# Float64 weights on a float32 chip: the sign set by a parametric ReLU instead of a masked OR

## The chip, the cores and the metric

The kernel runs on one core of a Trainium2 chip. The metric is device time of one execution in microseconds (us), the median over runs; before the change it is 1353.39 us over three runs (1353.15 to 1353.93). TensorE (PE in the rows) multiplies, VectorE (DVE) and ScalarE (ACT) do the elementwise work, SyncE (SP) issues the DMAs, GpSimd (POOL) does next to nothing. Each engine runs its own instructions strictly in order and waits on semaphores for the others.

## The reference

Two-way attention between a sequence and a small state, then two feed-forward layers. B = H = 8, S = 512, 32 state rows, head size 64; the layers see 4352 rows (512 + 32 rows for each of 8 batches), d_model 512, d_ff 2048.

```python
scores = scale * x @ state^T            # softmax over the state  -> xread = a @ state
scores2 = scale * state @ x^T           # softmax over the sequence -> sread = a2 @ x
x = concat(xread, sread) per head, laid out as rows of 512
h = x @ w_in;  x = (max(h, 0)**2) @ w_out              # first layer
h = x @ w_in2; x = elu(h) @ w_out2                     # second layer
```

The four weight matrices arrive as float64 (a float32 draw times a float64 factor). The chip's engines work on float32, so the kernel reads each float64 as two 32-bit words and builds a float32 from them.

## The kernel before, in words

**Stages.** The first layer runs batch by batch for six batches (`block`, 27.7 to about 505 us; it is written with plain products in three float32 pieces: a value is split into a high and a low part, and each product takes three matmuls, lines 158 to 160). Batches 6 and 7 are done as a pair with a seven-product scheme (`pair`, from about 505 us), then come the state rows and, from about 690 us, the whole second layer. Inside `block`, step i makes one tile h of 128 hidden rows (6 matmuls `h`), squares its ReLU (`relu2`, lines 469 to 474) and, two steps later, adds it into four accumulators (12 matmuls `acc`). `emit_m` folds the state into the first weight (`mp` matmuls of line 331, eight to a call) four times a batch.

**Conversion.** 64 pieces of 128 x 512 float64 (16 each of w1, v1, w2, v2) are converted beside this work. `load64` (line 195) loads a piece into one of four `raw` buffers. `convert` then runs: ACT scales the high word, read as a float32 of every second word, by 2^-112 (line 210); ACT scales the low word as an unsigned integer by 2^-29 (line 212); DVE clamps (line 214), shifts the bits left by three (line 215), which moves the float64 exponent's low bits and the mantissa into place and pushes the sign out; DVE adds the low word (line 217); and DVE ORs the sign bit of the high word back in with one scalar_tensor_tensor (line 219), which is the last reader of the `raw` buffer and the last writer of the converted piece. The pieces of w1 and v1 are all needed within batch 0; those of w2 and v2 are converted in batches 1 to 5 (`conv_pair`), where also sums of blocks (`sums`, lines 247 to 251) and splits (`put_split`, lines 260 and 261) are made and written to HBM.

**What sets the order.** `convert` and its callers are generators; each call of `next_conv` advances every conversion under way by one `yield`, starts one more, and when a conversion ends, issues the next load. In batch 0 there are two such calls a step. The layer that records the kernel then lists each engine's instructions in an order of its own, by dependencies and estimated costs; so taking one instruction out can reorder others far from it, on all engines, in both directions. Loads and stores all sit in the one queue of SP, in that recorded order.

**Start.** Until the first h matmul, PE runs the scores of batch 0, idle products that only keep it active (line 517), and the first `emit_m`, whose weight pieces come out of `convert`.

Of the kernel before, what the change touches and what calls it, by code (L numbers as in the profile page):

```python
# [9 lines left out]
F32 = mybir.dt.float32  # L10
# [3 lines left out]
AF = mybir.ActivationFunctionType  # L14
ALU = mybir.AluOpType
# [15 lines left out]
HF = FC // 2  # L31

CLAMP = 2.0 ** -96 * (2.0 - 2.0 ** -3 - 2.0 ** -22)
SIGN = -(1 << 31)
HI, LO = 0, 1
SINGLE = 6

# [67 lines left out]
def attn_mlp_kernel(ctx: ExitStack, tc: tile.TileContext, xt, xn, st, w1, v1, w2, v2, outx, outs):  # L105
# [13 lines left out]
    nc = tc.nc  # L119
# [49 lines left out]
    if True:  # L169
# [30 lines left out]
        def convert(name, i, out):  # L200

            t = raw.pop((name, i))
            low, high = t[:, :, 0], t[:, :, 1]
            bits = out.bitcast(I32)
            after = pace if name in ("w2", "v2") else gate
            with tc.issue_after(after[0].ins) if after else nullcontext():
                nc.scalar.activation(out=out, in_=high.bitcast(F32), func=AF.Copy, scale=2.0 ** -112)  # L210
            with tc.issue_after(gate[0].ins) if gate else nullcontext():
                nc.scalar.activation(out=low, in_=low.bitcast(U32), func=AF.Copy, scale=2.0 ** -29)
            yield
            nc.vector.tensor_scalar(out=out, in0=out, scalar1=CLAMP, scalar2=-CLAMP, op0=ALU.min, op1=ALU.max)
            nc.vector.tensor_single_scalar(out=bits, in_=bits, scalar=3, op=ALU.logical_shift_left)
            yield
            nc.vector.tensor_tensor(out=bits, in0=bits, in1=low, op=ALU.add)
            yield
            nc.vector.scalar_tensor_tensor(out=bits, in0=high, scalar=SIGN, in1=bits, op0=ALU.bitwise_and, op1=ALU.bitwise_or)

        def conv_w1(i):
            g, k = divmod(i, KC)
            if k % 2 == 0:
                half[g, k // 2] = wi_p.tile([P, 2, 512], F32, name=f"w1_{g}{k // 2}", tag="wi")
            t = half[g, k // 2]
            yield from convert("w1", i, t[:, k % 2])
            if k % 2:
                w1_t[g, k // 2] = t

        def conv_v1(f):  # L230
            v = conv_p["cv"].tile([P, 512], F32, name="cv", tag="cv")
            yield from convert("v1", f, v)
            d = wd["v1", f] = dram.tile([P, 512], F32, name=f"d_v1{f}", tag=f"d_v1{f}")
            nc.sync.dma_start(out=d, in_=v)
            t = wo_p.tile([P, 2, DM], F32R, name=f"v1_{f}", tag="wo")
            nc.scalar.activation(out=t[:, HI], in_=v, func=AF.Copy)
            yield
            nc.vector.tensor_tensor(out=t[:, LO], in0=v, in1=t[:, HI].bitcast(F32), op=ALU.subtract)
            wo_t["v1", f] = t
# [25 lines left out]
        def conv_pair(name, j):  # L265


            v = [conv_p["cv"].tile([P, 512], F32, name="cv", tag="cv") for _ in range(2)]
            for _ in zip_longest(convert(name, j, v[0]), convert(name, j + HF, v[1])):
                yield  # L270
            d = wd[name, j] = dram.tile([P, 2, 512], F32, name=f"d_{name}{j}", tag=f"d_{name}{j}")
            for r in range(2):
                nc.sync.dma_start(out=d[:, r], in_=v[r])
            for t in sums(v):
                yield
            w = wf[name, j] = dram.tile([P, NF, 2, 256], F32, name=f"f_{name}{j}", tag=f"f_{name}{j}")
            yield from put_split(w, ((1, v[0][:, :256].unsqueeze(1)), (2, v[1].rearrange("p (q f) -> p q f", q=2)),
                                     (2, t[:, :2]), (2, t[:, 2:])))
# [712 lines left out]
```

## Time and profile before

| what | value |
|---|---|
| median of 3 runs | 1353.39 us |
| span of the profiled execution, first to last instruction | 1350.5 us |
| mean granted TensorE clock | 0.997 |
| PE busy | 1327.5 us, 98% |
| DVE busy | 951.0 us, 70% |
| ACT busy | 839.5 us, 62% |
| DMA, mean over the span | 215 GB/s, 290.72 MB |

The page gives no time around the span of the profiled execution; the median of the runs is 2.9 us above the span. Busy shares are averages over stages that differ: DVE is at 70% over the whole, but busy 84.2 of 92.1 us in batch 0. PE at 98% leaves 23 us of the span in which it does nothing, and the question of any change off PE is how much of those 23 us it touches. The chain of work that ended last is 89% PE, 5% DMA, 3% DVE, 3% ACT.

### The profile page before, as it was taken

To read this page: it belongs to the slowest core of one execution; us is meant where nothing else is said; L and a number is where in the kernel's file an instruction comes from. 1 tells how busy PE (TensorE), PEld (TensorE's weight loads), DVE (VectorE), ACT (ScalarE), POOL (GpSimd) and SP (SyncE) were. 2 spreads that over 40 slices of the span, in tenths; PEclk is the share of its full clock that TensorE was granted. 3 is DMA by queue.
4 is the path that set the end of the run, shared out by engine and by line. 5 is a ranking of instruction groups with operands and counts; after the bars stand their busy time and mean duration, and the time that the engine had idled before them with its cause. 6 is when DMAs were issued, how large, how long until landed. Compare 5 with 4: busy or idle time off the path is not lost.

```text
span 1350.5 us, 19746 instructions
## 1 busy us (share of the span) xinstructions
PE 1327.5 (98%) x7064; PEld 1057.1 (78%) x7064; DVE 951.0 (70%) x1437; ACT 839.5 (62%) x1417; POOL 0.7 (0%) x6
## 2 busy tenths in 40 slices
PE   8989999999999999999999999999999999999998
PEld 6656777777777776778988888888888888888898
DVE  6997868686878865775576884579636884568644
ACT  5887758676777657644467843676446743666444
POOL 0000000000000000000000000000000000000000
PEclk9999999999999999999999999999999999999999
DMA  6988856575857424279077777767776777778732
GB/s 240 318 300 310 305 178 230 201 267 190 279 197 266 151 82 153 97 255 349 25 252 208 224 240 224 208 194 247 229 225 194 206 210 223 209 204 284 226 110 100
DMA packets 127729, 290.72 MB, mean 215 GB/s; under 512 B 13840, under 2 KB 22032, under 8 KB 124560
## 3 DMA queue, kind: packets, MB, share of 16 engines
q1 hardware_dynamic: 127632, 289.46, 66.3%
q8 instruction: 56, 0.92, 0.3%
q14 instruction: 41, 0.34, 0.1%
HBM read 212.86 MB, written 76.55 MB: 214 GB/s over the span
## 4 chain that ended last, share of the span: by engine, by line
PE 89%; DMA 5%; DVE 3%; ACT 3%; issue 1%; SPq 0%; ACTq 0%; DVEq 0%
PE x L43 16%; PE X L43 13%; PE z L43 8%; PE Z L43 6%; PE acc L158 6%; PE acc L159 6%; PE acc L160 6%; PE h L158 5%; PE h L159 4%; PE h L160 4%; PE y L43 4%; PE Y L43 3%; DMA raw_v<-in_v_dram 2%; PE mp L331 2%; PE hs L43 2%; PE as L43 2%
## 5 line engine op out<-in xcount | busy, mean ns | idle before, releaser
L163 ACT ACTIVATE gp<-g 128x1024 fp32r<-128x1024 f32 (+1 forms) x168 | 154.0, 917 | 146.0 <-PE x L43 69.5
L164 DVE TENSOR_TENSOR gp<-g,gp 128x1024 fp32r<-128x1024 f32 (+1 forms) x168 | 174.9, 1045 | 95.4 <-ACT gp L163 94.4
L43 PE MATMUL x<-gp,wr 128*128 128x512 f32 x960 | 223.5, 390 | 0.0
L43 PEld LDWEIGHTS x<-gp,wr 128*128 128x128 f32 x960 | 179.7, 188 | 39.4 <-ACT eu L71 1.9
L43 PE MATMUL X<-xf,wr 128*128 128x512 f32 x768 | 186.7, 390 | 0.0
L43 PEld LDWEIGHTS X<-xf,wr 128*128 128x128 f32 x768 | 143.4, 188 | 31.7 <-ACT u L748 1.3
L158 PE MATMUL acc<-gs,v 128*128 128x512 f32 x384 | 154.4, 402 | 3.8 <-DVE gs L474 1.9
L159 PE MATMUL acc<-gs,v 128*128 128x512 f32 x384 | 150.4, 392 | 0.0
L160 PE MATMUL acc<-gs,v 128*128 128x512 f32 x384 | 150.2, 392 | 0.0
L43 PE MATMUL z<-gp,wr 128*128 128x512 f32 x480 | 110.4, 389 | 0.0
L744 DVE SCALAR_TENSOR_TENSOR g<-r,g 128x512 f32<-128x512 f32 x96 | 63.9, 689 | 65.8 <-ACT r L743 65.8
L43 PEld LDWEIGHTS z<-gp,wr 128*128 128x128 f32 x480 | 90.1, 188 | 18.7
L158 PE MATMUL h<-at,m 128*128 128x512 f32 x256 | 103.0, 403 | 1.7 <-ACT r L469 1.7
L158 PEld LDWEIGHTS acc<-gs,v 128*128 128x128 f32 x384 | 72.0, 188 | 38.1 <-issue 15.9
L160 PE MATMUL h<-at,m 128*128 128x512 f32 x256 | 100.7, 395 | 0.5 <-ACT m L346 0.5
L159 PE MATMUL h<-at,m 128*128 128x512 f32 x256 | 101.0, 395 | 0.0
L43 PE MATMUL Z<-xf,wr 128*128 128x512 f32 x384 | 97.4, 389 | 0.0
L469 ACT ACTIVATE r<-h 128x512 f32<-128x512 f32 x96 | 57.1, 595 | 64.4 <-PE h L160 64.1
L742 ACT ACTIVATE r<-g 128x512 f32<-128x512 f32 x96 | 57.5, 625 | 57.5 <-DVE g L821 40.4
L160 PEld LDWEIGHTS acc<-gs,v 128*128 128x128 f32 x384 | 72.1, 188 | 19.8 <-issue 4.2
L159 PEld LDWEIGHTS acc<-gs,v 128*128 128x128 f32 x384 | 72.2, 188 | 18.6 <-issue 3.4
L43 PEld LDWEIGHTS Z<-xf,wr 128*128 128x128 f32 x384 | 72.1, 188 | 15.0
(145 smaller groups left out, 2173.6 us busy)
## 6 DMA issues: line engine op xcount, KB each, us to landing
wr<-f_v SPq DMA_DIRECT2D x256, 256.0 KB, 3.0
wr<-f_w SPq DMA_DIRECT2D x224, 256.0 KB, 2.9
f_v<-wf SPq DMA_DIRECT2D x40, 512.0 KB, 3.3
raw_w<-in_w_dram SPq DMA_DIRECT2D x32, 512.0 KB, 4.8
raw_v<-in_v_dram SPq DMA_DIRECT2D x32, 512.0 KB, 5.0
f_w<-wf SPq DMA_DIRECT2D x24, 512.0 KB, 2.8
xt<-in_xt_dram SPq DMA_DIRECT2D x8, 1024.0 KB, 6.9
xn<-in_xn_dram SPq DMA_DIRECT2D x8, 1024.0 KB, 6.1
```

Of the source, the lines that this page charges most:

```text
L43: nc.tensor.matmul(ps, wk[a], xk[b], start=start and k == 0 and i == 0, stop=last and k == len(w) - 1 and i == 2, skip_group_check=True)
L158: mm(ps, w[HI], x[LO], start=first, stop=False)
L159: mm(ps, w[HI], x[HI], start=False, stop=False)
L160: mm(ps, w[LO], x[HI], start=False, stop=last)
L163: copy = nc.scalar.activation(out=hi, in_=src, func=AF.Copy)
L164: nc.vector.tensor_tensor(out=lo, in0=src, in1=hi.bitcast(F32), op=ALU.subtract)
L331: mm(ps[e][32 * k:32 * k + 32, :], st_t[b][r, k, :], x(k, r), start=True, stop=True)
L469: pace[:] = [nc.scalar.activation(out=r, in_=ps, func=AF.Relu)]
L742: act(out=r, in_=h, func=AF.Relu, scale=-1.0)
L744: nc.vector.scalar_tensor_tensor(out=out, in0=r, scalar=-1.0, in1=h, op0=ALU.add, op1=ALU.max)
```

## The change

The scale-and-copy of the high word becomes a parametric ReLU: positive values pass, negative ones are multiplied by the slope `alpha` = 2^32. That adds 32 to the exponent field, which is one bit just above those that the shift by three keeps below the sign, so that the shift carries it into the sign's place. The lower clamp gets the same factor. The OR of line 219 and the `yield` ahead of it are dropped: a conversion is now two ACT instructions and three DVE instructions, and ends one `next_conv` call earlier. The number of ACT instructions, the loads, the buffers and the matmuls stay.

```diff
-SIGN = -(1 << 31)
+NEGATIVE = 2.0 ** 32
...
-                nc.scalar.activation(out=out, in_=high.bitcast(F32), func=AF.Copy, scale=2.0 ** -112)
+                nc.scalar.activation(out=out, in_=high.bitcast(F32), func=AF.Prelu, scale=2.0 ** -112, alpha=NEGATIVE)
...
-            nc.vector.tensor_scalar(out=out, in0=out, scalar1=CLAMP, scalar2=-CLAMP, op0=ALU.min, op1=ALU.max)
+            nc.vector.tensor_scalar(out=out, in0=out, scalar1=CLAMP, scalar2=-NEGATIVE * CLAMP, op0=ALU.min, op1=ALU.max)
             nc.vector.tensor_single_scalar(out=bits, in_=bits, scalar=3, op=ALU.logical_shift_left)
             yield
             nc.vector.tensor_tensor(out=bits, in0=bits, in1=low, op=ALU.add)
-            yield
-            nc.vector.scalar_tensor_tensor(out=bits, in0=high, scalar=SIGN, in1=bits, op0=ALU.bitwise_and, op1=ALU.bitwise_or)
```

In the changed kernel every line behind this function stands two lines higher (line 331 becomes 329, 469 becomes 467). The recorded order changes in many places; three of them follow.

On DVE, before the first h matmul (w_00 and w_01 are the first two halves of w1, t, m and z belong to the softmax of batch 0, atf is its transposed result). Before:

```order
L219 SCALAR_TENSOR_TENSOR w_00_154<-raw_w_146,w_00_154 128x512
L217 ISA w_01_207<-raw_w_148,w_01_207 128x1024
L382 TENSOR_REDUCE z_254<-t_178 128x32
L214 TENSOR_SCALAR w_01_207<-w_01_207 128x512
L383 TENSOR_SCALAR z_254<-z_254 128x32
L219 SCALAR_TENSOR_TENSOR w_01_207<-raw_w_148,w_01_207 128x512
L384 RECIPROCAL z_254<-z_254 128x32
L215 TENSOR_SCALAR w_01_207<-w_01_207 128x512
L385 TENSOR_TENSOR t_178<-t_178,z_254 128x1024
L217 ISA w_01_207<-raw_w_150,w_01_207 128x1024
L390 STREAM_TRANSPOSE atf_299<-t_178 128x1024
L219 SCALAR_TENSOR_TENSOR w_01_207<-raw_w_150,w_01_207 128x512
```

The same place on DVE in the changed kernel:

```order
L217 ISA w_01_209<-raw_w_148,w_01_209 128x1024
L214 TENSOR_SCALAR w_01_209<-w_01_209 128x512
L412 TENSOR_SCALAR z_181<-z_181 128x2
L215 TENSOR_SCALAR w_01_209<-w_01_209 128x512
L380 TENSOR_REDUCE z_255<-t_178 128x32
L217 ISA w_01_209<-raw_w_150,w_01_209 128x1024
L381 TENSOR_SCALAR z_255<-z_255 128x32
L413 RECIPROCAL z_181<-z_181 128x2
L382 RECIPROCAL z_255<-z_255 128x32
L383 TENSOR_TENSOR t_178<-t_178,z_255 128x1024
L388 STREAM_TRANSPOSE atf_295<-t_178 128x1024
```

Three scalar_tensor_tensors are gone, and the last write of w_01 (line 217 of raw_w_150) now stands ahead of the reciprocal, the product and the transpose of the softmax.

On PE, the third `emit_m` of batch 0 (eight mp_2 matmuls among the acc of batch 0). Before:

```order
L331 MATMUL mp_2_0_789<-w_20_489,st_142 32x512 x2
L160 MATMUL acc<-gs,v_5_610 128x512
L158 MATMUL acc<-gs,v_6_659 128x512
L159 MATMUL acc<-gs,v_6_659 128x512
L160 MATMUL acc<-gs,v_6_659 128x512
L331 MATMUL mp_2_1_790<-w_20_489,st_142 32x512 x2
L331 MATMUL mp_2_0_789<-w_21_615,st_142 32x512
L331 MATMUL mp_2_1_790<-w_21_615,st_142 32x512
L158 MATMUL acc<-gs,v_6_659 128x512
L159 MATMUL acc<-gs,v_6_659 128x512
```

The same call in the changed kernel:

```order
L160 MATMUL acc<-gs,v_5_590 128x512
L329 MATMUL mp_2_0_773<-w_20_483,st_142 32x512
L329 MATMUL mp_2_1_774<-w_20_483,st_142 32x512
L329 MATMUL mp_2_0_773<-w_20_483,st_142 32x512
L329 MATMUL mp_2_1_774<-w_20_483,st_142 32x512
L329 MATMUL mp_2_0_773<-w_21_605,st_142 32x512
L329 MATMUL mp_2_1_774<-w_21_605,st_142 32x512
L329 MATMUL mp_2_0_773<-w_21_605,st_142 32x512
L329 MATMUL mp_2_1_774<-w_21_605,st_142 32x512
L158 MATMUL acc<-gs,v_5_590 128x512
```

Before, the eight stand in three groups (the third, of two, comes 20 acc matmuls later); in the changed kernel in one.

On ACT, the end of batch 5 (wf is a split weight block of v2 on its way to HBM, o a finished accumulator, m the first operand of batch 6). Before:

```order
L260 ACTIVATE wf<-cv 128x256
L163 ACTIVATE at_5159<-atf_5036 128x512 x2
L260 ACTIVATE wf<-tf 128x2x256
L260 ACTIVATE wf<-cv 128x2x256
L503 ACTIVATE o<-acc 128x512
L260 ACTIVATE wf<-tf 128x2x256
L163 ACTIVATE m_10_5282<-mp_1_0_5272 128x512
L503 ACTIVATE o<-acc 128x512
L163 ACTIVATE m_11_5285<-mp_1_1_5273 128x512
L260 ACTIVATE wf<-tf 128x2x256
L630 ACTIVATE g_5260<-h_5253 128x512
```

The same place on ACT in the changed kernel:

```order
L467 ACTIVATE r<-h 128x512
L163 ACTIVATE at_5111<-atf_5003 128x512
L469 ACTIVATE g<-r 128x512
L471 ACTIVATE gs<-r 128x512
L163 ACTIVATE at_5111<-atf_5003 128x512
L501 ACTIVATE o<-acc 128x512 x2
L163 ACTIVATE m_10_5218<-mp_1_0_5208 128x512
L163 ACTIVATE m_11_5221<-mp_1_1_5209 128x512
L628 ACTIVATE g_5196<-h_5189 128x512
```

Before, six splits of v2 stand behind the last relu of batch 5; in the changed kernel the last split stands eight relus ahead of it.

## Rows read from the trace of the kernel before

**Rows 1.** Windows by stage: busy us (instructions) of each engine, PEclk, DMA share, GB/s.

```profile
27.70:34.30 6.60, 5.67 (x79) 4.12 (x77) 5.73 (x12) 6.57 (x14) 0.00 (x0) 0.76 0.46 156
34.30:126.40 92.10, 85.08 (x431) 53.93 (x432) 84.20 (x167) 76.11 (x140) 0.00 (x0) 1.00 0.92 313
126.40:484.00 357.60, 357.31 (x2147) 270.11 (x2145) 274.43 (x522) 245.71 (x459) 0.00 (x0) 1.00 0.63 220
484.00:511.00 27.00, 24.45 (x196) 16.21 (x196) 16.66 (x31) 15.71 (x31) 0.00 (x0) 0.96 0.41 156
...
120.00:130.00 10.00, 10.00 (x45) 8.26 (x44) 5.72 (x12) 4.26 (x8) 0.00 (x0) 1.00 0.97 372
```

**Rows 2.** Waits of PE in batch 0, longest first: us, times, longest.

```profile
PE acc L158 <- DVE gs L474: 1.9, 2, 1.5
PE acc L158 <- ACT raw_w L212: 1.8, 1, 1.8
PE h L158 <- ACT r L469: 1.7, 2, 0.9
```

**Rows 3.** Waits of SP's queue, 0 to 126.4 us.

```profile
SPq L195 <- DVE w L219: 51.3, 16, 8.1
```

**Rows 4.** Chain that ended last, in order of time: start us, us, what.

```profile
41.54 5.64 DMA raw_v<-in_v_dram
...
93.29 6.99 DMA raw_v<-in_v_dram
```

**Rows 5.** Line 219 in batch 0: ns min/median/max, first and last start.

```profile
L219 DVE SCALAR_TENSOR_TENSOR cv<-raw_v,cv x15: 678/683/698, 35.0 to 114.4; 128x512 int32<-128x512 int32 x15
L219 DVE SCALAR_TENSOR_TENSOR w<-raw_w,w x11: 648/682/685, 38.4 to 102.9; 128x512 int32<-128x512 int32 x11
```

**Rows 6.** Timeline of the start: start us, us, engine, line, instruction.

```profile
19.77 2.50 PE L517 MATMUL idle<-ident 128*128 128x128 f32 x20
20.81 0.68 DVE L219 SCALAR_TENSOR_TENSOR w<-raw_w,w 128x512 int32<-128x512 int32 x1
21.41 0.34 DVE L384 RECIPROCAL z<-z 128x32 f32<-128x32 f32 x1
24.84 0.65 DVE L219 SCALAR_TENSOR_TENSOR w<-raw_w,w 128x512 int32<-128x512 int32 x1
25.55 1.05 PE L331 MATMUL mp<-w,st 64*32 64x512 f32 x4 [2.30 <-DVE w L219]
27.60 0.67 ACT L210 ACTIVATE cv<-raw_v 128x512 f32<-128x512 f32 x1
27.73 0.63 PE L158 MATMUL h<-at,m 128*128 128x512 f32 x1
33.65 0.59 ACT L469 ACTIVATE r<-h 128x512 f32<-128x512 f32 x1
34.30 0.50 PE L158 MATMUL h<-at,m 128*128 128x512 f32 x1 [0.93 <-ACT r L469]
```

**Rows 7.** Timeline of PE: part of an emit_m, and the matmul behind it.

```profile
68.78 1.05 PE L331 MATMUL mp<-w,st 64*32 64x512 f32 x4 [0.21 <-DVE mx L363]
69.76 0.50 PE L160 MATMUL acc<-gs,v 128*128 128x512 f32 x1
```

**Rows 8.** Timeline of the change from batch 5 to the pair.

```profile
504.94 1.09 PE L331 MATMUL mp<-w,st 64*32 64x512 f32 x16
505.98 0.63 ACT L260 ACTIVATE wf<-tf 128x512 fp32r<-128x512 f32 x1 [2.37 <-DMA f_v<-wf]
507.99 2.81 PE L331 MATMUL mp<-w,st 64*32 64x512 f32 x16 [1.96 <-DVE m L164]
510.73 0.79 PE L158 MATMUL h<-at,m 128*128 128x512 f32 x1
```

**Rows 9.** Line 210 by form: ns min/median/max, first and last start.

```profile
L210 ACT ACTIVATE cv<-raw_v x32: 644/666/690, 27.6 to 463.3; 128x512 f32<-128x512 f32 x32
L210 ACT ACT_TABLE_LOAD  x1: 1283/1283/1283, 0.7 to 0.7; - x1
```

## The prediction

> **What bounds the kernel now.** The page first: PE is busy 98% of the span, so only the time in which PE stands still, or runs at the lower clock, can be won. The windows by stage say where that is [rows 1]. From 126.4 to 484 us PE is busy 357.31 of 357.60 us: nothing to win there, although DVE is busy for 274 us and loses work. From 34.3 to 126.4 us, which is batch 0, PE stands for 92.10 - 85.08 = 7.0 us; DVE is busy 84.2 of those 92.1 us (91%), ACT 76.1, and the DMA engines 92% at 313 GB/s. From 27.7 to 34.3 PE's clock is 0.76 on average, between the 2.4 and 1.2 GHz levels. From 484 to 511 PE stands 2.6 us, and the clock falls to 0.96. Behind that no conversion is left.
>
> The waits of PE in batch 0 [rows 2] name DVE (1.9 us) and ACT (1.8 and 1.7 us), and smaller ones below. The wait that matters stands one step further back: SP's loads of raw pieces wait 51.3 us, in 16 waits, for line 219 [rows 3], which is what frees a raw buffer. The chain of waits then runs through five such loads, the first of 5.64 us at 41.54, the longest of 6.99 us at 93.29 [rows 4]. So in batch 0 a loop of load, ACT, DVE, load sets the pace, and line 219 is its last step. The timeline of the start [rows 6] shows the same in small: the last quarter of the first emit_m (25.55) waits 2.30 us for line 219.
>
> **The change part by part.**
>
> *The instructions themselves.* Gone: 64 scalar_tensor_tensors of 0.68 us [rows 5]; back to back on DVE one takes a slot of 0.60 us (20.81 to 21.41) [rows 6]. 26 of them lie in batch 0: 26 x 0.60 = 15.6 us off 84.2 us leaves DVE at 68.6. The other half lies where PE is at 100%, and is worth nothing there. Line 210 stays one ACT instruction of the same shape; nothing in the trace runs a parametric ReLU. I take the 0.666 us of the copy that it replaces [rows 9], at no cost; the bounds are the relu of line 469 at 0.59 us [rows 6] below (64 times 0.08, on ACT) and a second pass, twice 0.666, above, which is a rival.
>
> *The start, 2.0 us.* Before, the last write of w_01 ended just ahead of 25.55. In the new order it stands before the reciprocal, the product and the transpose of the softmax; with the strike of the two slots ahead of it, it is done near 21.3. It isn't what ends last then: PE runs the idle products from 19.77, and their 2.4 us (19.77 to 22.2) [rows 6] now stand in front of the last quarter, which starts at 22.2 instead of 25.55. Of these 3.35 us most is used up behind it: ACT now takes the four copies of m before the two operand copies. From 27.60 to 33.65 ACT did eleven pieces, 0.55 us each. The first two m end 2.05 us after the quarter started, as before (25.55 to 27.60): 24.25; two more m and two operand copies, with 0.35 us of waiting for the product between: 26.8; DVE's rest of the first half is done near 27.0, where the first h starts (27.73 before). ACT then has nine pieces instead of eleven ahead of the first relu: 26.8 + 9 x 0.55 = 31.75 against 33.65. The third h waits for that relu, so PE is 34.30 - 32.3 = 2.0 us ahead; the products for the state read (1.1 us), which stood among the h, now fill the wait in front. Bounds: 0.7 (first h alone) and 3.35 (the whole advance). I take the clock there as it was.
>
> *Batch 0, the holes, 5.0 us.* The 7.0 us of standing: holes that wait for DVE lose their cause, since DVE falls from 91 to about 75% of the stretch; that is 1.9 for gs, and three of 0.2 to 0.5 us that stand lower in the same view, 2.8 in all. The other 4.2 us wait for ACT, which isn't busier and not freer; but ACT itself stands behind raw loads, and a raw buffer comes free one DVE slot and one call of next_conv sooner. I take half: 2.1, together 4.9, say 5.0. What is late next: the loads. 313 GB/s over 92.1 us is 28.8 MB; if the stretch shrinks to 85 us the same bytes need 339 GB/s, and right behind, from 120 to 130 us, 372 are reached [rows 1]. The SP order also gives way: ahead of the first result of batch 0 stood ten stores p_v of 0.5 MB, and now six, so 2 MB are moved behind it. Bounds: 0 and 7.0.
>
> *Batch 0, the emit_m, 2.0 us.* A part of an emit_m takes as long as a whole: two of eight matmuls hold PE from 68.78 to 69.76 [rows 7], 0.98 us (the trace counts two passes each), and all eight do so for 1.09 us at 504.94 [rows 8]. In the recorded order batch 0 has twelve such groups before and nine now: the third emit_m in one group instead of three, that of batch 1 in one instead of two. Three groups are 2.9 us; as some of them stood in a hole that would be there anyway, I take 2.0. Bounds 0 and 2.9.
>
> *From batch 5 to the pair, 4.0 us.* At 505.98 ACT waits 2.37 us for a store of a split weight, and the copies of m stand in order behind it; PE runs dry, its next emit_m waits 1.96 us and, at half clock, takes 2.81 instead of 1.09 us [rows 8]: 1.96 + 1.72 = 3.7, and the h behind it, the first of 0.79 us, lose some 0.7 more by my estimate: 4.4. In the new order all splits are through eight relus earlier, so no such wait stands there, and the second emit_m isn't in front of the first h either. Bounds: 0 (another wait in its place) and 5.1 with the small stops ahead of it. I take 4.0.
>
> *The rest, 0.* Between 126.4 and 484 us the conversions end earlier, with PE full and DVE and ACT at 77 and 69%: covered. If the cover broke, the store waits of SP would show on PE, which waits 0.3 us there now.
>
> Sum: 2.0 + 5.0 + 2.0 + 4.0 = 13.0 us. The profiled execution's span is 1350.5, so 1337.5; the median lies 2.9 us above that span, which I carry over: **1340.4 us**. All lower bounds together give 0.7 us, 1352.7; all upper ones 3.35 + 7.0 + 2.9 + 5.1 = 18.4 us, 1335.0.
>
> **A rule weighed: the table load.** The trace has one activation table load, 1283 ns, at 0.7 us [rows 9]; the recorded order of the changed kernel has one such row too, in the same place, so copy, relu, square, exponential and parametric ReLU sit in one set. The Trainium skill ("ScalarE activation tables: per-element evaluation and per-set limits", section "What a function is on this engine") says that two functions of different sets are one load apart and that two of one set need no switch. By that rule, with one set the sum is unchanged; with two sets it would be the rival below.
>
> **The rivals.**
>
> *The loads take over in batch 0.* DMA engines at 92% speak for it [rows 1], the store order against it. Then neither holes nor groups are worth anything: 2.0 + 4.0 = 6.0 us, **1347.4**.
>
> *Nothing moves.* The reordering opens as many holes as it closes: the products of the state read now stand before the first h and wait for DVE, and an emit_m in one group must wait for its last quarter of weights before its first matmul. Within 2.7 us (0.2%, about what a measurement of this kernel can tell from no change) of 1353.4. Against it: the DVE wait is gone for good, and the stop at 506 us is not made by chance of order alone.
>
> *Slower: the parametric ReLU takes two passes on ACT.* Place: line 210. Price: 0.666 us each. In batch 0, 24 of them add 16.0 us to ACT's 76.1: exactly the 92.1 us of the stretch, so ACT would be the bound, and being in order it could not fill every gap; with the 69 to 83% that it reaches in these stretches now [rows 1], I put batch 0 at 8 us longer. At the start five lie on ACT's path to the first relu and before: 3.3 us. Minus the 4.0 us at batch 5: 1353.4 + 8 + 3.3 - 4.0 = **1360.7**. It decides from about 0.3 us extra a piece on, where 24 x 0.3 = 7.2 us eat the gain of batch 0. For it speaks only that no row shows the function; against it that copy, relu and square of this width all lie between 0.59 and 0.68 us. The Trainium skill ("ScalarE: Activation LUTs", section "ACT is a hardware spline evaluator") gives one element per cycle and lane whatever the function, which would be, as an estimate from that page, the same time as the copy; no run before shows it for this one.
>
> *The ReLU sits in another table set than the exponential.* Then each of 19 alternations between line 210 and the exponentials in the new order costs one load of 1.283 us [rows 9]; four lie in the start, 5.1 us, the rest mostly in ACT's idle time: 1340.4 + 5.1 = **1345.5**. The recorded order speaks against it.
>
> **How the numbers follow.** Forecast 0.62 (its own range 1336 to 1345); loads take over 0.22; nothing moves 0.08; two passes, or another hole that costs over 2.7 us, 0.07; table loads 0.01. The predicted time is 1340.4. The range takes in the loads' case and nearly the upper bounds of the terms: 1335 to 1349.5, leaving out about 0.17. Faster by over 0.2%: 0.62 + 0.22 + 0.01 = 0.85; same 0.08; slower 0.07.
>
> **What would show it.** Right: batch 0's first accumulator copied near 117 instead of 126.4 us; DVE at 75 to 80% in that stretch and no longer the releaser of SP's loads; line 210 at 0.67 us; no wait on a store near 495 us, and the clock at 1.00 there. Wrong: line 210 longer than 0.7 us; PE in batch 0 with as many stops as before, behind raw loads; a new stop where batch 5 hands over; or a stop between 130 and 480 us, where there is none now.

## The result, and the profile after

The changed kernel takes 1342.2 us, median of four runs (1341.26 to 1343.03), against 1353.66 for the kernel before, run beside it (four runs, 1353.15 to 1354.03). The ratio is 0.9918, with a 95% interval of 0.9905 to 0.9931: 11.1 us faster (9 to 13). Predicted were 1340.4 us, 13.0 less. Its profiled execution took 1342.72 us, with a span of 1340.9.

From the head of the page after, the busy time of each engine:

```profile
PE 1321.0 (99%) x7064; PEld 1056.0 (79%) x7064; DVE 914.5 (68%) x1373; ACT 836.6 (62%) x1417; POOL 0.7 (0%) x6
```

DVE has lost 36.5 us, PE 6.5 and the span 9.6. The marks that the prediction used, in the profiled executions (us):

| stretch | before | after | gain | predicted |
|---|---|---|---|---|
| start of the span to the third h of batch 0 | 34.30 | 33.05 | 1.25 | 2.0 |
| third h to the first accumulator copied | 92.06 | 82.86 | 9.2 | 5.0 + 2.0 |
| that copy to the first `mp` of the pair | 378.58 | 383.89 | -5.3 | 0 |
| that `mp` to the first h of the pair | 5.79 | 1.99 | 3.8 | 4.0 |
| the rest | 839.77 | 839.11 | 0.65 | 0 |

The windows of the changed kernel by stage, with the columns of [rows 1]: the end of the start, batch 0, batches 1 to 5, and a stretch inside the third:

```profile
28.10:33.05 4.95, 4.07 (x15) 2.31 (x15) 4.95 (x13) 4.92 (x10) 0.00 (x0) 1.00 0.89 295
33.05:115.90 82.85, 79.95 (x426) 54.20 (x427) 71.51 (x140) 74.95 (x140) 0.00 (x0) 1.00 0.92 318
115.90:499.80 383.90, 379.18 (x2310) 285.46 (x2309) 268.41 (x516) 257.90 (x486) 0.00 (x0) 1.00 0.61 220
130.00:480.00 350.00, 345.70 (x2080) 260.45 (x2078) 252.28 (x487) 238.28 (x450) 0.00 (x0) 1.00 0.64 230
```

In batch 0 PE stands 82.85 - 79.95 = 2.9 us, where it stood 7.0, and DVE is at 71.51 of 82.85 (86%). The DMA engines stay at 92%, at 318 GB/s, in a stretch that is nine microseconds shorter. That does not show that they were no limit: by rate times time they moved 26.3 MB in it instead of 28.8, and six stores `p_v` of 0.5 MB are issued ahead of the first result instead of ten. From 130 to 480 us, where before PE stood 0.3 us, it now stands 4.3.

The waits in batch 0, SP's queue first (0 to 116 us; from, releaser: us, times, longest), which answer to [rows 3]:

```profile
SPq L195 <- DVE w L217: 24.1, 14, 6.0
SPq L232 <- DVE cv L217: 19.3, 9, 3.3
```

The loads still wait for DVE, but half as long (24.1 for 51.3 us). A part of their wait has only moved to the stores of converted pieces, which stand in the same queue (line 232, 234 before); before, these waited:

```profile
SPq L234 <- DVE cv L219: 9.7, 5, 3.3
```

All waits of the queue for DVE up to the first accumulator copied add up to 84.9 us before and 72.2 us now. And PE's waits, 33.05 to 115.9 us, which answer to [rows 2]:

```profile
PE acc L158 <- DVE gs L472: 1.7, 2, 0.9
PE mp L329 <- DVE t L364: 0.5, 1, 0.5
PE srt L422 <- DVE m L164: 0.5, 1, 0.5
PE h L158 <- ACT r L467: 0.2, 1, 0.2
```

Before, these stood below the three of [rows 2], with two more of 0.2 us for DVE:

```profile
PE mp L345 <- ACT m L344: 1.0, 1, 1.0
PE mp L331 <- DVE stf L426: 0.5, 1, 0.5
PE h L160 <- ACT m L346: 0.5, 1, 0.5
```

The 1.8 us behind a raw load are gone and the 1.7 behind relus are down to 0.2; the wait for gs is nearly as before. Added up by releaser, PE's waits for ACT fell from 5.0 to 0.2 us, and those for DVE stayed, 2.8 and 2.9 us. (These sums are up to 0.9 us above the time PE stands between the marks, since the first wait begins ahead of the mark.)

Where PE's busy time fell in that stretch is told by the groups of PE instructions (busy us, mean ns):

```profile
L329 PE MATMUL mp<-w,st 64*32 64x512 f32 x62 | 10.9, 600 | 0.7 <-DVE t L364 0.5 <-DVE w L217 0.2
L329 PE MATMUL sc<-xt,st 64*32 64x512 f32 x16 | 1.1, 601 | 0.0
```

The same groups of the kernel before, 34.3 to 126.4 us:

```profile
L331 PE MATMUL mp<-w,st 64*32 64x512 f32 x64 | 12.9, 600 | 0.9 <-DVE stf L426 0.5 <-DVE mx L363 0.2 <-DVE w L219 0.2
L331 PE MATMUL sc<-xt,st 64*32 64x512 f32 x16 | 2.1, 601 | 0.0
```

The scores of batch 1, in one group instead of two, take 1.0 us less, which the prediction had not counted. The `mp` matmuls take 2.0 us less, but these are not all the same ones: two of the 64 now stand ahead of the third h, in the wait for the first relu:

```profile
31.88 1.01 PE L329 MATMUL mp<-w,st 64*32 64x512 f32 x2 [0.71 <-DVE w L217]
```

So 1.0 us of the 2.0 left the stretch with them, and fewer groups brought the other 1.0.

The end of batch 5, in the timeline after, which answers to [rows 8]:

```profile
499.80 1.09 PE L329 MATMUL mp<-w,st 64*32 64x512 f32 x16
501.14 0.60 ACT L501 ACTIVATE o<-acc 128x512 f32<-128x512 f32 x1 [2.68 <-DMA x2d<-o]
501.79 0.51 PE L158 MATMUL h<-at,m 128*128 128x512 f32 x1 [0.90 <-ACT o L501]
```

The 2.81 us `mp` no longer stands ahead of that h (the second group of 16 now starts at 510.25 and takes 1.09 us), and h starts 1.99 us after the first `mp` instead of 5.79. A wait on a store is still there, 2.68 us on ACT for an output buffer; it costs PE 0.90 us.

The new stop, at the end of batch 1. First ACT's timeline of the changed kernel, then PE's first h behind it:

```profile
190.09 0.60 ACT L501 ACTIVATE o<-acc 128x512 f32<-128x512 f32 x1 [2.57 <-PE acc L160]
194.83 0.69 ACT L212 ACTIVATE raw_w<-raw_w 128x512 int32<-128x512 uint32 x1 [4.14 <-DMA raw_w<-in_w_dram]
196.52 0.60 ACT L501 ACTIVATE o<-acc 128x512 f32<-128x512 f32 x1 [1.00 <-DMA x2d<-o]
197.01 0.59 ACT L467 ACTIVATE r<-h 128x512 f32<-128x512 f32 x1
...
197.66 0.50 PE L158 MATMUL h<-at,m 128*128 128x512 f32 x1 [1.79 <-ACT r L467]
```

Between two accumulator copies stands the low word of a conversion (line 212), and its load isn't there for 4.14 us. Behind it the second copy waits another 1.00 us, since its output buffer is still being stored, and only then comes the relu for which PE's h matmuls stand. Nothing binds line 212 to a place behind that relu: for w2 and v2 line 210 is bound behind the latest relu by `issue_after(after[0].ins)`, line 212 isn't. The other long stop of PE between 130 and 480 us, at the end of batch 3, comes behind ACT too, but another instruction: between two copies ACT waits for the store of a split weight.

```profile
346.36 0.63 ACT L258 ACTIVATE wf<-tf 128x512 fp32r<-128x512 f32 x1 [1.95 <-DMA f_v<-wf]
...
350.83 0.50 PE L158 MATMUL acc<-gs,v 128*128 128x512 f32 x1 [1.36 <-DVE gs L472]
```

The function itself, line 210 by form, which answers to [rows 9]:

```profile
L210 ACT ACTIVATE cv<-raw_v x32: 649/664/776, 27.4 to 414.5; 128x512 f32<-128x512 f32 x32
L210 ACT ACT_TABLE_LOAD  x1: 1283/1283/1283, 0.7 to 0.7; - x1
```

A parametric ReLU takes what the copy took, and there is one table load (the other two forms of the line have medians of 682 and 671 ns, 666 ns both before).

### The profile page after: what moved, and what is told of

Its sections match the earlier page's. It is cut to its first block, busy times and chain, and to the rows that moved or that the text cites. A ratio compares the mean times of both kernels' runs of the same rounds, so it can differ in the third digit from the quotient of the medians.

```text
span 1340.9 us, 19689 instructions
## 1 busy us (share of the span) xinstructions
PE 1321.0 (99%) x7064; PEld 1056.0 (79%) x7064; DVE 914.5 (68%) x1373; ACT 836.6 (62%) x1417; POOL 0.7 (0%) x6
## 4 chain that ended last, share of the span: by engine, by line
PE 88%; ACT 3%; DMA 3%; DVE 3%; issue 1%; SPq 0%; DVEq 0%; ACTq 0%
PE x L43 16%; PE X L43 13%; PE z L43 8%; PE Z L43 6%; PE acc L158 6%; PE acc L160 6%; PE acc L159 6%; PE h L158 4%; PE h L159 4%; PE y L43 4%; PE h L160 4%; PE Y L43 3%; PE mp L329 2%; PE hs L43 2%; PE as L43 2%
## 5 line engine op out<-in xcount | busy, mean ns | idle before, releaser
L472 DVE TENSOR_TENSOR gs<-g,gs 128x512 fp32r<-128x512 f32 x96 | 66.1, 689 | 29.5 <-ACT gs L471 28.5
L159 PEld LDWEIGHTS acc<-gs,v 128*128 128x128 f32 x384 | 72.2, 188 | 15.2 <-issue 1.7
```

The costliest lines, as they stand in the source:

```text
L159: mm(ps, w[HI], x[HI], start=False, stop=False)
L472: nc.vector.tensor_tensor(out=gs[:, LO], in0=g, in1=gs[:, HI].bitcast(F32), op=ALU.subtract)
```

## The experiments

Ratios are to the kernel before, run beside each. First, which part of the change brings which part of the gain.

**The parametric ReLU alone** (built on the kernel before: the OR and its `yield` stay).

```diff
-                nc.scalar.activation(out=out, in_=high.bitcast(F32), func=AF.Copy, scale=2.0 ** -112)
+                nc.scalar.activation(out=out, in_=high.bitcast(F32), func=AF.Prelu, scale=2.0 ** -112, alpha=NEGATIVE)
...
-            nc.vector.tensor_scalar(out=out, in0=out, scalar1=CLAMP, scalar2=-CLAMP, op0=ALU.min, op1=ALU.max)
+            nc.vector.tensor_scalar(out=out, in0=out, scalar1=CLAMP, scalar2=-NEGATIVE * CLAMP, op0=ALU.min, op1=ALU.max)
```

> The parametric ReLU stays, and the scalar_tensor_tensor of the sign and the yield ahead of it are put back (the OR sets a bit that is set already). If the gain comes from DVE's dropped slot and the earlier end of a conversion, and the ReLU costs on ACT what the copy cost, this is the kernel before again: 1353.6 us, 1352.5 to 1355, line 210 at 0.66 to 0.68 us. If the ReLU costs more on ACT, it is slower than before: over 1356. If the ReLU itself brought the gain, it is at 1342.

Measured: 1352.56 us, ratio 0.9994 (0.9984 to 1.0004). Line 211, which is line 210 here:

```profile
L211 ACT ACTIVATE cv<-raw_v x32: 642/666/741, 28.1 to 465.1; 128x512 f32<-128x512 f32 x32
```

The function costs nothing and brings nothing by itself; the rival of two passes falls.

**The `yield` kept** (built on the changed kernel: the OR is gone, but a conversion ends one call later, as before).

```diff
             nc.vector.tensor_tensor(out=bits, in0=bits, in1=low, op=ALU.add)
+            yield
```

> The changed kernel with the last yield of a conversion put back, the scalar_tensor_tensor still dropped: DVE's work as in the changed kernel, the pace of the generators (and so of the loads in the recorded order) as before. If DVE's slot is what counts: about 1344 us, batch 0's first accumulator copied by 118 us. If the pace of the generators is what counts: about 1351, and the copy near 125 us.

Measured: 1347.18 us, ratio 0.9949 (0.9934 to 0.9964). PE's timeline of the hand-over:

```profile
501.11 1.09 PE L330 MATMUL mp<-w,st 64*32 64x512 f32 x16
503.67 2.06 PE L330 MATMUL mp<-w,st 64*32 64x512 f32 x16 [1.47 <-DVE m L164]
505.65 0.50 PE L158 MATMUL h<-at,m 128*128 128x512 f32 x1
```

The first accumulator is copied at 115.8 us (table below), as in the changed kernel; the stop at the hand-over is back. The time is that of neither case named beforehand.

**The OR kept, the `yield` dropped** (built on the changed kernel).

```diff
             nc.vector.tensor_tensor(out=bits, in0=bits, in1=low, op=ALU.add)
+            nc.vector.scalar_tensor_tensor(out=bits, in0=high, scalar=SIGN, in1=bits, op0=ALU.bitwise_and, op1=ALU.bitwise_or)
```

> The changed kernel with the scalar_tensor_tensor put back right behind the addition, without a yield between: DVE's work as before, the pace of the generators as in the changed kernel. If DVE's slot is what counts: about 1351 us, the first accumulator of batch 0 copied near 124 us. If the pace counts: about 1344, and near 118 us.

Measured: 1353.21 us, ratio 1.0000 (0.9988 to 1.0012). The same view:

```profile
507.97 1.09 PE L331 MATMUL mp<-w,st 64*32 64x512 f32 x16
509.93 0.50 PE L159 MATMUL h<-at,m 128*128 128x512 f32 x1 [0.87 <-ACT o L503]
```

The mirror image: batch 0 as before (first copy at 126.2 us), the hand-over clean. So the dropped instruction brings the whole of batch 0, and the dropped `yield` the hand-over. Neither the median nor the marks of batches 1 to 5 are sums of the two, though (table below).

**The OR twice for w1 and v1** (built on the kernel before).

```diff
             nc.vector.scalar_tensor_tensor(out=bits, in0=high, scalar=SIGN, in1=bits, op0=ALU.bitwise_and, op1=ALU.bitwise_or)
+            if name in ("w1", "v1"):
+                nc.vector.scalar_tensor_tensor(out=bits, in0=high, scalar=SIGN, in1=bits, op0=ALU.bitwise_and, op1=ALU.bitwise_or)
```

> The kernel before with the OR of the sign done twice for w1 and v1 (the second changes nothing): 32 more slots of 0.6 us on DVE, 26 of them in batch 0. If DVE's slots are what batch 0 waits for, batch 0 grows by most of 26 x 0.6 = 15.6 us, as DVE was at 91% there: 1353 + 10 to 16 = 1366, line 219 the more the releaser of SP's loads. If the loads or ACT set the pace and line 219 only frees the buffer late, the growth is that delay alone, under 5 us: 1357.

Measured: 1373.55 us, ratio 1.0141 (1.0115 to 1.0167), more than the 10 to 16 us named beforehand. Its window of batch 0, from the third h to the first copy, and the longest wait of PE there:

```profile
37.90:148.83 110.93, 94.68 (x430) 57.35 (x431) 100.56 (x195) 79.00 (x139) 0.00 (x0) 0.92 0.80 271
```

```profile
PE acc L158 <- DVE gs L476: 7.6, 4, 4.5
```

The first accumulator is copied at 148.8 us, 22.5 later than before. All 32 added slots lie ahead of it: DVE is busy 126.5 us up to there instead of 108.0. In the changed kernel it is 92.1, 16.0 less, and the copy comes 10.5 us earlier; so DVE time costs more when added than it gains when dropped. The DMA engines fall to 80% and 271 GB/s: in this kernel they follow DVE's pace, and don't set it. The clock of PE fell to 0.92 there, so the surplus over the 18.5 us is not DVE alone.

Two things go with line 219 and no run parts them from the DVE slot: the raw buffer that comes free one instruction earlier, and the order of the stores. Every kernel here that drops the line for w1 and v1 has six stores `p_v` issued ahead of the first result, and every one that keeps it has ten to twelve. The four fewer, 2 MB, are some 6.6 us at the 318 GB/s of that stretch, by my estimate, and with the DMA engines at 92% before and after it is open how much of batch 0's gain is theirs.

Next, whence the 5.3 us lost in batches 1 to 5.

**The change for w1 and v1 only** (the conversions of batch 0; w2 and v2 keep copy, OR and `yield`).

```diff
+            new = name in ("w1", "v1")
...
+            if not new:
+                yield
+                nc.vector.scalar_tensor_tensor(out=bits, in0=high, scalar=SIGN, in1=bits, op0=ALU.bitwise_and, op1=ALU.bitwise_or)
```

> The change for w1 and v1 alone (all converted in batch 0); w2 and v2 are converted as before. My account: batch 0 keeps its 10 us; batches 1 to 5 have PE as full as before (the 5 us lost there in the changed kernel don't come about), and the stop where batch 5 hands over is back (4 us): 1353.6 - 10 + 0 to 1 = 1344. Rival, that the loss in batches 1 to 5 follows from batch 0 being early, whatever w2 and v2 do: 1348. Rival, that the late conversions brought the gain: 1352.

Measured: 1347.37 us, ratio 0.9953 (0.9936 to 0.9971). The window and the stop at the end of batch 1:

```profile
130.00:480.00 350.00, 345.91 (x2061) 259.96 (x2060) 265.04 (x508) 235.60 (x440) 0.00 (x0) 1.00 0.62 219
```

```profile
194.21 0.69 ACT L214 ACTIVATE raw_w<-raw_w 128x512 int32<-128x512 uint32 x1 [4.07 <-DMA raw_w<-in_w_dram]
```

The conversions of batches 1 to 5 are as they were, and PE still stands 4.1 us there: the stops come with the shorter batch 0 even without the faster late conversions. The account given beforehand (1344 us, PE as full as before) missed, and the first rival (1348) was met.

**The change for w2 and v2 only** (`new = name in ("w2", "v2")`).

> The change for w2 and v2 alone; w1 and v1 are converted as before. Batch 0 should stay as it was (first accumulator copied at 126 us), and the hand-over behind batch 5 be clean, as in the changed kernel. My account: 1353 - 4 = 1349. If the stops at the ends of batches 1 to 4 come from the shorter late conversions, 1 to 5 us of that are lost again: 1350 to 1353; if they come from batch 0 being early, PE stands under 2 us between 130 and 480.

Measured: 1353.0 us, ratio 1.0002 (0.9992 to 1.0012). The hand-over is clean (h 1.96 us after the first `mp`), but reached later; no net gain, where the account given beforehand had 1349. So faster late conversions cost something ahead of the hand-over by themselves, 3.3 us in the table below, of which 0.9 us are stops (PE stands 1.8 us in that stretch, 0.9 before).

**The low word bound like the high word** (built on the changed kernel).

```diff
-            with tc.issue_after(gate[0].ins) if gate else nullcontext():
+            with tc.issue_after(after[0].ins) if after else nullcontext():
                 nc.scalar.activation(out=low, in_=low.bitcast(U32), func=AF.Copy, scale=2.0 ** -29)
```

> The changed kernel, with the scaling of the low word of w2 and v2 (line 212) bound behind the last relu, as line 210 already is, so that it can't stand on ACT ahead of the next relu while its load is under way. If that line is what opens the stops at the ends of batches 1 to 4: 3 us faster than the changed kernel, PE standing under 2 us between 130 and 480. Rival, that the two o buffers (a store of a finished accumulator not yet out) make the stops: within 1 us of the changed kernel.

Measured: 1343.36 us, ratio 0.9931 (0.9911 to 0.995): no gain over the changed kernel's 0.9918, which is the rival's case. The same place on ACT:

```profile
196.51 0.60 ACT L501 ACTIVATE o<-acc 128x512 f32<-128x512 f32 x1 [4.94 <-DMA x2d<-o]
```

The wait at the raw load is gone, and the second copy waits as long for the store that had stood hidden behind it.

**Four buffers for the finished accumulators** (built on the changed kernel).

```diff
-    o_p = pool("o", 2)
+    o_p = pool("o", 4)
```

> The changed kernel with four buffers o for finished accumulators instead of two. If the wait of the third copy for the store of the first makes the stops at the ends of batches, and holds up the first h of the pair at 501.8 us (0.9 us): 3 us faster than the changed kernel. Rival, line 212 behind a raw load: within 1 us of the changed kernel, since ACT then still stands 4 us ahead of the second copy at 190 us.

Measured: 1341.91 us, ratio 0.9916 (0.9901 to 0.9932): no gain either, again the rival's case. The same place:

```profile
193.05 0.68 ACT L212 ACTIVATE raw_w<-raw_w 128x512 int32<-128x512 uint32 x1 [3.59 <-DMA raw_w<-in_w_dram]
```

**Both repairs** (the last two edits together, on the changed kernel).

> Both repairs together. If the stops between 116 and 500 us are made by these two in-order waits on ACT, PE stands under 2 us there: 4 to 5 us faster than the changed kernel, near 1337.5. If they are moved on to another wait: no faster than the better one of the two alone.

Measured: 1337.52 us (1336.28 to 1339.0), ratio 0.9887 (0.987 to 0.9905): the fastest version, 4.7 us below the changed kernel by the medians, 4.2 by the ratios. The window, ACT at the end of batch 1, and all that PE waits for from 116 to 520 us:

```profile
130.00:480.00 350.00, 349.01 (x2144) 263.92 (x2146) 254.12 (x488) 244.38 (x461) 0.00 (x0) 1.00 0.64 228
```

```profile
189.93 0.60 ACT L501 ACTIVATE o<-acc 128x512 f32<-128x512 f32 x1 [0.76 <-PE acc L160]
192.04 0.60 ACT L467 ACTIVATE r<-h 128x512 f32<-128x512 f32 x1 [1.51 <-PE h L160]
```

```profile
PE sc L329 <- DVE m L164: 0.6, 1, 0.6
PE tp L399 <- DVE m L164: 0.4, 1, 0.4
```

The second copy and the relu now wait for PE alone, and PE stands 1.0 us of 350. The stop at the end of batch 3 is gone too, though neither edit touches the split that stood in front of it; the edits reorder other instructions as well.

**Both repairs on the kernel before** (the same two edits).

> The kernel before with the two repairs (line 212 bound behind the last relu for w2 and v2, four o buffers), without the change. The repairs mend stops that stand, in the kernel before, only in batch 5's hand-over, if anywhere: 1353 - 0 to 2 us. If they bring the same 4.7 us here as in the changed kernel, they have nothing to do with the change: 1348.5.

Measured: 1351.46 us, ratio 0.9982 (0.997 to 0.9994): 2.4 us, about half of what they bring to the changed kernel, and none of it in batches 1 to 5 (378.9 us in the table, 378.6 without them).

The marks of all runs, each from one profiled execution (us). "Stood" is 350 less PE's busy time from 130 to 480 us. In the three kernels with 1.0 under "`mp` to h", only 2 or 4 of the 16 `mp` records stand ahead of that h; the others come behind it.

| kernel | first copy | copy to `mp` of the pair | `mp` to h | stood |
|---|---|---|---|---|
| before | 126.4 | 378.6 | 5.8 | 0.3 |
| ReLU alone | 127.6 | 379.2 | 4.9 | 0.8 |
| `yield` kept | 115.8 | 385.3 | 4.5 | 6.0 |
| OR kept | 126.2 | 381.8 | 2.0 | 2.2 |
| w1, v1 only | 115.4 | 386.0 | 3.5 | 4.1 |
| w2, v2 only | 126.7 | 381.9 | 2.0 | 1.4 |
| OR twice | 148.8 | 378.9 | 4.6 | - |
| changed | 115.9 | 383.9 | 2.0 | 4.3 |
| low word bound | 116.8 | 383.6 | 2.0 | 3.6 |
| four buffers | 114.7 | 383.1 | 1.0 | 3.3 |
| both repairs | 114.4 | 378.8 | 1.0 | 1.0 |
| both, on before | 128.4 | 378.9 | 1.0 | 0.6 |

Three things are to be seen. Every kernel in which batch 0 ends early and not both repairs are in takes 383 to 386 us for batches 1 to 5; with both it takes 378.8, as it did before the change. Wherever the late conversions lose their `yield` and batch 0 is as it was, the hand-over gains 3.8 us and the stretch ahead of it loses 3.2 or 3.3: that pair of numbers is why the `yield` alone brings nothing. And with a shorter batch 0 and the old late pace, the loss is largest (6.7 and 7.4 us). So the loss has two sources, the shorter batch 0 and the dropped `yield` of the late conversions, and they don't add up.

Not all of the loss is stops. From the first copy to that `mp` PE stands 0.9 us before and 4.7 in the changed kernel, and is busy 377.7 and 379.2 us with the same number of matmul records: 3.8 + 1.5 us. With both repairs it is 1.0 us and 377.8.

## Why the prediction was right, and where it failed

*The start, 2.0 predicted, 1.25 on the clock of the span.* The timeline after, which answers to [rows 6]:

```profile
10.03 1.09 PE L329 MATMUL sc<-xt,st 64*32 64x512 f32 x16 [1.11 <-DMA xt<-in_xt_dram]
20.66 2.50 PE L515 MATMUL idle<-ident 128*128 128x128 f32 x20
23.09 1.05 PE L329 MATMUL mp<-w,st 64*32 64x512 f32 x4
28.12 0.50 PE L158 MATMUL h<-at,m 128*128 128x512 f32 x1
33.05 0.50 PE L158 MATMUL h<-at,m 128*128 128x512 f32 x1 [0.15 <-ACT r L467]
```

The last quarter of `emit_m` follows the idle products without a wait, as forecast (23.09, of which 0.9 us are the later scores). Scores started 0.9 us later in this execution, since xt landed at 10.03 instead of 9.14 us; counted from the scores, the third h came after 23.02 instead of 25.16 us, 2.1 us earlier. The start of the scores varied from 8.7 to 10.03 us over the profiled runs; counted from it, the third h came after 23.0 us in all six kernels that drop the OR for w1 and v1. The first h came only 0.5 us earlier on that count (28.12 for 27.73 us); the rest of the 2.1 us lies between it and the third. One step was wrong in kind: the prediction took the clock as it was, and it rose from 0.76 to 1.00 in that stretch. It gave little back, because the third h waits for the first relu anyway: the kernel before with both repairs has the old order there, happened to run it at 1.00, and needed 6.62 us for what took 6.57 us at 0.76.

```profile
27.81:34.43 6.62, 4.76 (x79) 2.97 (x77) 5.68 (x12) 6.59 (x14) 0.00 (x0) 1.00 0.44 157
```

*Batch 0, 5.0 + 2.0 predicted, 9.2 measured.* The instruction was right: without line 219 it happens, with it it doesn't, and with twice as many it goes the other way. PE stands 4.1 us less, with 5.0 predicted, but the split behind the 5.0 was wrong: the 2.8 us of holes that wait for DVE were to vanish, and half of the 4.2 us that wait for ACT; measured, DVE's stayed at 2.9 us and nearly all of ACT's went. That the two came out near 5 in sum is luck; what held is the reason given for ACT, that it stands behind raw loads whose buffers come free sooner: its waits for raw loads in the stretch fell from 10.3 to 2.6 us. The 2.0 us of the `emit_m` groups were met by luck as well: 1.0 us came from fewer groups, not 2.9, since the third `emit_m` ran in two parts after all and three groups took 1.43 to 1.67 us instead of 1.05, and 1.0 us from a part that moved ahead of the mark. Left out were 1.0 us for the scores of batch 1, 0.4 us for two `srt` products that now stand ahead of the mark as well, and the edges: an acc or h next to a group or a stop holds PE for 0.31 to 0.34 us instead of 0.23, 33 times before and 22 now in the timelines, 1.1 us. DVE lost 12.7 us in the stretch, not 15.6; it is at 86% rather than 75 to 80, and still releases the loads, half as long. The rival in which the loads take over did not come in its strong form, since the stretch shrank by a tenth; but the rate did not rise to the 339 GB/s that the prediction named either, it stayed at 318 with 2.5 MB less to move, and whether the DMA engines hold the stretch now is not shown.

*The hand-over, 4.0 predicted, 3.8 measured.* Right in size. The reason given (all splits are through eight relus earlier) is the dropped `yield`, as the runs with one of the two edits show, and has nothing to do with the OR's time. One reading in its sum was off: the 2.81 us of the old `mp` are not all half clock. Its last 14 weight loads start 0.86 us after it, behind a second wait for `m`, and the granted clock was 0.87 from 508 to 509 us and 0.50 only behind that.

```profile
508.85 0.22 PEld L331 LDWEIGHTS mp<-w,st 64*32 64x32 f32 x14 [0.72 <-DVE m L164]
```

*"The rest, 0": the step that failed, by 5.3 us.* The prediction said that between 126.4 and 484 us the conversions end earlier, with PE full: "covered". It looked for a break of the cover at the store waits of SP, and named a stop between 130 and 480 us as a sign of being wrong; that sign came. The break came on ACT, at the ends of batches, where one in-order instruction that waits for a DMA stands ahead of the relu that PE needs; DVE's and ACT's shares say nothing on that. Before, the same kinds of wait were there, and PE had work beside them: ACT's waits from 116 to 500 us of the kernel before, then of the changed one:

```profile
ACT raw_w L212 <- DMA raw_w<-in_w_dram: 8.4, 8, 2.4
```

```profile
ACT raw_w L212 <- DMA raw_w<-in_w_dram: 14.9, 9, 4.1
```

The longest grew from 2.4 to 4.1 us. That the loss hangs on where such instructions stand on ACT is shown by the two repairs: at the end of batch 1 each alone only brings up the other (383.6 and 383.1 us), both give back 5.1 of the 5.3. How the 5.1 divide is not shown, since the stop at the end of batch 3 stood behind another wait and went with them. Why a shorter batch 0 makes the waits longer is not settled: each variant has an order of its own and other loads in flight, and no run held the order while it moved the time. Nor is it shown where the 3.2 us go that the dropped `yield` costs ahead of the hand-over in the kernels with the old batch 0; 1.1 to 1.9 us of them stand in the "stood" column.

*The sum.* 1.25 + 9.2 - 5.3 + 3.8 + 0.65 = 9.6 us of span; the errors of +2.2 and -5.3 partly cancel. The step from span to median was 1.1 us off: every run here has 1.7 to 1.9 us around its span, so that the 2.9 carried over held a profiled execution 1.1 us faster than its median. The profiled execution after was 0.5 us slower than its own, so the marks, which compare these two, give 9.6 us where the medians are 11.5 apart.

*The other rivals.* Two passes and another table set are excluded by line 210 at 0.664 to 0.682 us at the median and the single table load. "Nothing moves" describes the kernel with the `yield` dropped and the OR kept, 1.0000, and for the reason it gave: the order opens as much as it closes.

## What to carry to other kernels

Taking work off an engine that isn't the bottleneck paid here where that engine is the last link of a loop through a few buffers (91% busy, with the loads waiting for it), and not where the bottleneck was full. When such a stage gets shorter, look at the places where an in-order engine waits for a DMA ahead of the instruction that feeds the bottleneck: bind these instructions behind it, and give the buffers for both waits; here repairing one only showed the other. An instruction and the pacing step beside it are two changes; try them apart before putting the gain down to either. And a mark that comes out as predicted can hold two errors: compare the waits behind it too.

## What was not expected of the hardware

Thirty-two more slots on DVE up to the first copy cost 22.5 us where 18.5 us of DVE time were added, and the granted clock of PE fell from 1.00 to 0.92 in batch 0, where PE now stood for up to 4.5 us at a time. At the start the granted clock from the first to the third h was 1.00 (2.4 GHz) in every kernel in which the last quarter of `emit_m` comes earlier; in those with the old order, in which that quarter waits 2.30 or 2.31 us, it was 0.76, 0.59, 0.68 and once 1.00. So the same stop was followed by a lower clock in three profiled executions of four, and no run shows what decides it. A parametric ReLU with slope 2^32 had the time of a copy (664 for 666 ns at the median).
